# An FFT filter and an ELU block: Z on 128 partitions, its first rows asked for early, weights cast by transfers, late loads in two parts

## The chip, the cores and the metric

The kernel runs on one core of one Trainium2 chip. Its engines are TensorE (PE; PEld in the profile is its weight load), VectorE (DVE), ScalarE (ACT), GpSimd (POOL) and SyncE (SP). Each takes its instructions strictly in its own order. DMAs are issued from SP's queue or from POOL's. The metric is the device time of one execution in microseconds (us); lower is better.

## The reference

```python
X = np.fft.rfft(x, axis=1)                     # x: 8 x 3008 x 256
Yr = Xr @ w_r - Xi @ w_i + b_r                 # 256 x 256 weights
Yi = Xr @ w_i + Xi @ w_r + b_i
Y = shrink(Yr, 0.01) + 1j * shrink(Yi, 0.01)   # sign(v) * max(|v| - 0.01, 0)
y = np.fft.irfft(Y, n=3008, axis=1)            # -> 24064 tokens x 256
h = y @ w_in                                   # 256 x 2048
g = np.where(h > 0, h, np.exp(np.minimum(h, 0)) - 1)
out = g @ w_out                                # 2048 x 256
```

## The kernel before

3008 is 47 times 64, so each transform is done in two matrix stages with constant matrices M1 to M4 that the kernel computes itself at the start (iotas on POOL, range reduction on DVE, Sin on ACT). A batch goes through these units:

- **A**: six units per batch. M1 times x (three tiles `xts[ci]`, two units each); the result `A` is written to a buffer `DA` in DRAM and read back in another layout as `Z`.
- **X**: eight units, eight matmuls each (`M2`, 96 columns) over `Z`. Unit u takes group g = u // 2 of eight slots of Z and half dt = u % 2 of the features. The result is evacuated to `XT` by ACT or DVE. `Z` lies on 96 partitions: (j, h, c), j from 0 to 23; it has one buffer.
- **M**: `XT` times `wcat_r` and `wcat_s` (the complex weights side by side), bias, and the shrinking to `Y`, on DVE with POOL, or in the first batch on ACT with DVE by turns. There, a bias is either added from `bias_bc` by DVE or put into PSUM by a matmul of ones with `bias_p`, which holds the bias as three bf16 parts in rows 0, 32 and 64.
- **B**: M3 times `Y`, written to `DB` in DRAM and read back as `Bs`.
- **Y**: M4 times `Bs`, giving `yT`, the transposed tokens.

Tokens then go through `front` (h = `w_in_s` times `yT`, then Exp on ACT), `elu`/`finish_elu` (POOL and DVE make `gT`), and `back` (`gT` times `w_out_r`, summed over 16 tiles of the hidden size in `ps_o`). One step i of the main loop is one pair of hidden tiles for 512 tokens: 8 pairs per block, 376 steps. The order is written out by hand: `plan(b)` puts the units of batch b+1 (and A of batch b+2) between the steps of batch b, and PE, busy with `front` and `back`, runs them in that order. The first ten steps (`FILL`) use single PSUM banks and carry the units A 1 to 5 of batch 1 and the rest of the first batch's Y.

The opening, before step 0, is the first batch alone, in this order: constants and six A units (with `idle_pe` matmuls, whose results aren't used, between and after them), Z in four slices of eight slots, eight X units, then M by halves (`first_M`, q = 3, 4, 5, 0, 1, 2) with B 3, 4, 5, 0 between them. For B 0 to 2 of the first Bs, a turn inside PE (`turn_B`, `turn_back`) replaces the way through DRAM; rows 48 to 96 of that Bs come by a DMA. `split_B`, `first_Y` and step 0 follow.

The bulk loads: x of batch 1 (three loads of 1 MB) and half of `w_out` (1 MB) go out on POOL's queue behind `gate(Z_of[0][:, 8, 0:1])`, a tiny POOL copy that waits for the second slice of Z; the other half of `w_out` behind a gate on the first `Bs`. `w_in` comes in four quarters as float32 on SP's queue, and DVE scales each to bf16 by 2/S (L727), half a quarter at a time, between the units. `w_r` and `w_i` come as float32 on SP's queue and POOL makes the four parts of `wcat_r` and `wcat_s` of them (L659 to L662).

PSUM in the opening: `pre2` has two double banks (A, X, B), `pre1` four single banks (M and the idle matmuls).

## Time and profile before

| | us |
|---|---|
| median of 3 runs (907.12 to 908.94) | 907.5 |
| the profiled execution, whole | 911.15 |
| the profiled execution, span | 909.3 |
| busy in the span: PE / DVE / ACT / POOL | 887.4 / 719.7 / 696.1 / 325.1 |
| first X matmul | 22.38 |
| first M matmul | 31.71 |
| first B matmul | 39.03 |
| first turn-back matmul | 51.01 |
| first matmul of step 0 | 53.88 |
| first X matmul of batch 1 | 77.11 |

The times of events are from the start of the span. A line such as `PE xps L183 <- DVE XT L126: 1.7, 1, 1.7` reads: PE stood idle before the instruction of line 183 that writes `xps`, until DVE's instruction of line 126 that writes `XT` was done; 1.7 us in all, one time, the longest 1.7. In the chain of waits, each line is a start, a length, and the engine, tile and line that the end of the work can be followed back through. In a table by stretches, the columns are the stretch, its length, an engine's busy time (and its instructions), the granted PE clock as a share of full speed, the share of the DMA engines' time, and GB/s. L126 and L128 are the copies of the helper `evac`, on DVE and ACT.

### The profile page before, as it was taken

What the parts mean: (1) busy time and instruction counts of PE and PEld (TensorE: products, weight loads), DVE (VectorE), ACT (ScalarE), POOL (GpSimd) and SP (SyncE); (2) the same over time, 40 slices, a digit from 0 to 9 for tenths busy, and PEclk for the clock granted to TensorE, in tenths of its full rate; (3) what the DMA queues carried; (4) which work ended last, traced back from release to release, by engine and by line L of the source; (5) the groups of instructions that cost most, each with busy time, mean ns of one, the idle gap of its engine ahead of it and who ended that gap; (6) DMA issues with size and microseconds to landing.
All of it is one profiled execution on the core that took longest, in us unless ns stands there. A gap on an engine that the chain in (4) does not pass through costs nothing.

```text
span 909.3 us, 17311 instructions
## 1 busy us (share of the span) xinstructions
PE 887.4 (98%) x6664; PEld 654.4 (72%) x6767; DVE 719.7 (79%) x908; ACT 696.1 (77%) x869; POOL 325.1 (36%) x457
## 2 busy tenths in 40 slices
PE   8898999999999999999999999999999999999997
PEld 3467667876678766886678766787667867777776
DVE  8687778887788778897788877888778877778776
ACT  6577778778878778787787788878887877767664
POOL 7552441233321341405404154032332134443665
PEclk9799999999999999999999999999999999999999
DMA  8977225721283214732266032752228011231011
GB/s 270 296 216 237 74 71 157 238 70 48 70 243 128 71 47 136 195 112 76 64 194 200 26 93 60 210 172 62 78 65 237 25 43 51 73 91 48 24 47 47
DMA packets 90655, 106.06 MB, mean 117 GB/s; under 512 B 5302, under 2 KB 81340, under 8 KB 87212
## 3 DMA queue, kind: packets, MB, share of 16 engines
q1 hardware_dynamic: 84316, 77.42, 30.5%
q0 software_dynamic: 5968, 27.26, 9.0%
q8 instruction: 53, 0.87, 0.4%
q10 hardware_dynamic: 288, 0.26, 0.1%
q14 instruction: 30, 0.25, 0.1%
HBM read 55.12 MB, written 49.81 MB: 115 GB/s over the span
## 4 chain that ended last, share of the span: by engine, by line
PE 85%; DVE 4%; ACT 3%; DMA 3%; issue 2%; POOL 1%; SPq 0%; DVEq 0%; ACTq 0%; POOLq 0%
PE ps_o L945 34%; PE hps L871 33%; PE mps L200 9%; PE bps L252 2%; PE yps L420 2%; PE xps L183 2%; PE aps L150 2%; DMA Z<-DA 1%; DVE gT L915 1%; DVE Et L926 1%; ACT Et L889 1%; ACT Et L892 1%; DMA xt<-in_x_dram 1%; ACT Bz L265 1%; DMA Bs<-DB 0%
## 5 line engine op out<-in xcount | busy, mean ns | idle before, releaser
L945 PE MATMUL ps_o<-w_out_r,gT 128*128 128x256 f32 x3008 | 475.3, 301 | 0.7 <-DVE gT L913 0.7
L945 PEld LDWEIGHTS ps_o<-w_out_r,gT 128*128 128x128 f32 x3008 | 402.9, 189 | 49.8 <-DVE osb L957 1.4
L871 PE MATMUL hps<-yT,w_in_s 128*128 128x512 bf16 (+7 forms) x1613 | 371.9, 350 | 5.9 <-DVE gT L913 1.0
L913 DVE SCALAR_TENSOR_TENSOR gT<-Et,hps 128x512 fp32r<-128x512 f32 (+1 forms) x268 | 220.2, 851 | 74.4 <-POOL Et L924 38.1
L915 DVE SCALAR_TENSOR_TENSOR gT<-hps,Et 128x1024 fp32r<-128x1024 f32 x190 | 232.4, 1223 | 14.9
L871 PEld LDWEIGHTS <-w_in_s 128*128 128x128 bf16 x1728 | 141.8, 98 | 129.0 <-issue 21.5
L924 POOL TENSOR_SCALAR Et<-Et 128x512 f32<-128x512 f32 x204 | 121.5, 615 | 230.9 <-ACT Et L887 218.6
L892 ACT ACTIVATE Et<-hps 128x1024 f32<-128x1024 f32 x190 | 195.8, 1031 | 9.7 <-PE hps L871 3.5
L926 DVE TENSOR_SCALAR Et<-Et 128x1024 f32<-128x1024 f32 x190 | 131.5, 692 | 47.9 <-ACT Et L892 40.4
L218 POOL TENSOR_SCALAR clip<-yb 128x512 f32<-128x512 f32 x84 | 51.7, 615 | 314.5 <-DVE yb L210 282.3
L887 ACT ACTIVATE Et<-hps 128x512 f32<-128x512 f32 x182 | 98.9, 595 | 62.4 <-PE hps L871 60.9
L889 ACT ACTIVATE Et<-hps 128x1024 f32<-128x1024 f32 x84 | 86.3, 1027 | 71.5 <-PE hps L871 70.0
L219 POOL TENSOR_TENSOR Y<-yb,clip 128x512 bf16<-128x512 f32 x84 | 107.2, 1277 | 7.0
L890 ACT ACTIVATE Et<-Et 128x1024 f32<-128x1024 f32 x84 | 88.8, 1058 | 2.6
L210 DVE TENSOR_TENSOR yb<-mps,bias_bc 128x512 f32<-128x512 f32 x89 | 61.3, 689 | 37.2 <-PE mps L200 24.8
L128 ACT CAST XT<-xps 128x768 bf16<-128x768 f32 x61 | 48.8, 799 | 17.9 <-PE xps L183 17.9
L200 PE MATMUL mps<-wcat_r,XT 128*128 128x512 bf16 x180 | 56.7, 391 | 0.8 <-ACT Bz L265 0.3
L200 PE MATMUL mps<-wcat_s,XT 128*128 128x512 bf16 x182 | 55.9, 385 | 0.7
L200 PEld LDWEIGHTS <-XT 128*128 128x128 bf16 x384 | 31.2, 99 | 30.9 <-issue 2.7
L128 ACT CAST A<-aps 128x1024 bf16<-128x1024 f32 x42 | 42.5, 1014 | 13.1 <-PE aps L150 11.7
L128 ACT CAST yT<-yps 128x752 bf16<-128x752 f32 x56 | 44.2, 789 | 10.4 <-PE yps L420 10.3
L265 ACT CAST Bz<-bps 128x1024 bf16<-128x1024 f32 x45 | 45.1, 1001 | 2.7 <-PE bps L252 2.7
(146 smaller groups left out, 466.7 us busy)
## 6 DMA issues: line engine op xcount, KB each, us to landing
xt<-in_x_dram POOLq DMA_DIRECT2D x21, 1024.0 KB, 7.1
out_dram<-osb SPq DMA_DIRECT2D x158, 128.0 KB
Bs<-DB SPq DMA_DIRECT2D x30, 384.0 KB
DA<-A SPq DMA_DIRECT2D x20, 512.0 KB
DB<-Bz SPq DMA_DIRECT2D x20, 512.0 KB
Z<-DA SPq DMA_DIRECT2D x7, 1152.0 KB
Z<-DA SPq DMA_DIRECT2D x11, 384.0 KB
xt<-in_x_dram POOLq DMA_DIRECT2D x6, 512.0 KB, 5.9
```

The lines of the kernel that those rows point to most:

```text
L128: nc.scalar.copy(dst, src)
L200: nc.tensor.matmul(ps, lhsT=XT[:, dt, c, o : o + P], rhs=wm[:, dt, :], start=(not biased and m == 0 and dt == 0), stop=(m == 1 and dt == 1),)
L219: nc.gpsimd.tensor_tensor(Y_of[b, q][:, i, :], yb, clip[:], ALU.subtract)
L871: nc.tensor.matmul(hps[s][:, c0:c1] if early else hps[:, s, c0:c1], lhsT=w_in_s[:, dt, ft * P : ft * P + P], rhs=yT_of[b][:, dt, t0 : t0 + ...
L887: nc.scalar.activation(E_[:, s], hps[:, s], AF.Exp)
L889: nc.scalar.activation(E_, hps[:], AF.Relu, scale=-1.0)
L892: nc.scalar.activation(E_, hps[:], AF.Exp)
L913: nc.vector.scalar_tensor_tensor(o, e, -1.0, h, ALU.add, ALU.max)
L915: nc.vector.scalar_tensor_tensor(o, h, 0.0, e, ALU.max, ALU.add)
L924: nc.gpsimd.tensor_scalar(E_[s], E_[s], 1.0, 0.0, ALU.min, ALU.max)
L926: nc.vector.tensor_scalar(E_, E_, 1.0, -1.0, ALU.min, ALU.add)
L945: nc.tensor.matmul(po[q][:, i_ % 2, :], lhsT=gT[:, s, i_ * P : i_ * P + P], rhs=w_out_r[:, ft, :], start=(ft == 0 and i_ % 2 == 0), stop=( ...
```

## The change

- `Z0` has 128 partitions and is the one Z of all batches. Of rows 0 to 31 (j from 0 to 7, which the first third of A writes), slot groups 0 and 2 go to partitions 0 to 31, and groups 1 and 3 to partitions 96 to 127, by two DMAs of their own (`load_Z(b, None, None)`); rows 32 to 95 go by the loads as before. Partitions 0 to 31 of groups 1 and 3 are cleared once by ACT. X units of odd groups use all 128 partitions, those of even groups 96; M2 is computed for 128 partitions.
- In the first batch, the two early DMAs are issued right behind the last A write, ahead of its landing; in the others likewise, behind the last A write's issue.
- `w_r` and `w_i` are cast to bf16 by DMAs of POOL's queue behind a gate on the last A tile, and `wcat_s` is made from `wcat_r`. POOL's operations for M4 move behind their issue. `w_in` comes in two halves, cast by DMAs of POOL's queue into `w_in_s`; the factor 2/S goes into M4's weights, and `scale_w_in` is gone.
- The bulk loads: behind the Z gate `w_in`'s first half, x(1,0), x(1,1), `w_out`'s first half; behind the Bs gate `w_in`'s second half, `w_out`'s second half, x(1,2).
- The bias is split on eight partitions by POOL, goes through DRAM (`bpd`) to the rows of `bias_p`, and `bias_bc` is made by a matmul and an ACT copy.
- X of the first batch has three double banks; DVE takes units 2, 4 and 7 instead of 1, 4 and 7; w3's subtraction is behind unit 2, the Abs behind unit 7. 34 idle matmuls instead of 40 ahead of X, three instead of eight within it. In the first batch, M takes the feature half 0 of both weights first.

```diff
@@ -55,7 +55,7 @@
...
     M1 = constp.tile([P, P], F32R, name="M1")
-    M2 = constp.tile([2 * NR, NS, 2, 2 * K1], BF16, name="M2")
+    M2 = constp.tile([P, NS, 2, 2 * K1], BF16, name="M2")
     M3 = constp.tile([P, K1 // 2, 2, P], BF16, name="M3")
...
@@ -84,9 +84,9 @@
     xtp = ctx.enter_context(tc.tile_pool(name="xtp", bufs=1))
...
     ctx.enter_context(tc.manual_schedule())
-    first, second = ExitStack(), ExitStack()
-    pre2 = first.enter_context(tc.tile_pool(name="pre2", bufs=2, space=bass.MemoryType.PSUM))
-    pre1 = first.enter_context(tc.tile_pool(name="pre1", bufs=4, space=bass.MemoryType.PSUM))
+    zeroth, first, second = ExitStack(), ExitStack(), ExitStack()
+    pre2 = zeroth.enter_context(tc.tile_pool(name="pre3", bufs=3, space=bass.MemoryType.PSUM))
+    pre1 = zeroth.enter_context(tc.tile_pool(name="pre0", bufs=2, space=bass.MemoryType.PSUM))
...
@@ -166,10 +166,17 @@
...
-        if b not in Z_of:
-            Z_of[b] = zp.tile([2 * NR, NS, D], BF16, name="Z", tag="Z")
+        Z_of[b] = Z0
         dv = DA_of[b].rearrange("j (h c s) d -> (j h c) s d", h=2, c=2)
-        nc.sync.dma_start(Z_of[b][:, s0:s1, :], dv[:, s0:s1, :])
+        if s0 is None:
+            for t in range(2):
+                dst, src = (
+                    v.rearrange("p (g t s) d -> p g t (s d)", t=2, s=8)[:, :, t]
+                    for v in (Z0[96 * t : 96 * t + 32], dv[0:32])
+                )
+                nc.sync.dma_start(dst, src)
+        else:
+            nc.sync.dma_start(Z0[32:96, s0:s1, :], dv[32:96, s0:s1, :])
...
         g, dt = u // 2, u % 2
@@ -180,9 +187,10 @@
         psv = ps[:].rearrange("p a (k j) -> p (a k) j", j=P)
...
             k = 8 * g + kk
+            r = slice(0, P if g % 2 else 2 * NR)
             nc.tensor.matmul(
-                psv[:, kk, 0 : 4 * K1], lhsT=Z[:, k, dt * P : dt * P + P],
-                rhs=M2[:, k].rearrange("p c m -> p (c m)"), start=True, stop=True,
+                psv[:, kk, 0 : 4 * K1], lhsT=Z[r, k, dt * P : dt * P + P],
+                rhs=M2[r, k].rearrange("p c m -> p (c m)"), start=True, stop=True,
             )
...
@@ -195,12 +203,14 @@
         o = (2 * q + i) * P
...
             nc.tensor.matmul(ps, lhsT=busy[:, 0:P], rhs=bias_p[:], start=True, stop=False)
-        for m, (c, wm) in enumerate(((0, wcat_r), (1, wcat_s))):
-            for dt in range(2):
-                nc.tensor.matmul(
-                    ps, lhsT=XT[:, dt, c, o : o + P], rhs=wm[:, dt, :],
-                    start=(not biased and m == 0 and dt == 0), stop=(m == 1 and dt == 1),
-                )
+        todo = [(c, dt) for c in range(2) for dt in range(2)]
+        if b == 0:
+            todo.sort(key=lambda z: z[1])
+        for c, dt in todo:
+            nc.tensor.matmul(
+                ps, lhsT=XT[:, dt, c, o : o + P], rhs=(wcat_r, wcat_s)[c][:, dt, :],
+                start=(not biased and (c, dt) == (0, 0)), stop=((c, dt) == (1, 1)),
+            )
         if i == 0:
...
@@ -434,15 +444,17 @@
         for _ in range(n):
...
-    brow, rest = (wk3.tile([P, 2 * D], F32, name="yb", tag="yb") for _ in range(2))
-    nc.vector.memset(brow[:], 0.0)
-    for o, bv in ((0, b_r), (D, b_i)):
-        for k in range(3):
-            nc.sync.dma_start(
-                brow[32 * k : 32 * k + 1, o : o + D],
-                bass.AP(tensor=bv.tensor, offset=bv.offset, ap=[[0, 1], [1, D]]),
-            )
+    nc.vector.memset(bias_p[:], 0.0)
+    bpd = dram.tile([3, 2 * D], BF16, name="bpd", tag="bpd")
+    Z0 = zp.tile([P, NS, D], BF16, name="Z")
     idle_pe(9)
+    gatep = ctx.enter_context(tc.tile_pool(name="gatep", bufs=2))
+
+    def gate(src):
+
+        t = gatep.tile([P, 1], F32, name="gate", tag="gate")
+        nc.gpsimd.tensor_copy(t[0 : src.shape[0], :], src)
+
     xts = []
...
         pcol = iota("pcol", [P, 1], [[0, 1]], cm=1)
+        offs = row("offs", [P, 1])
+        nc.gpsimd.memset(offs[:], 0.0)
+        nc.gpsimd.memset(offs[2 * NR : P, :], float(-NR))
+
+        def clear(g):
+            nc.scalar.activation(
+                Z0[0:32, 8 * g : 8 * g + 8, :].rearrange("p s d -> p (s d)"),
+                busy[0:32, 0:1].to_broadcast([32, 8 * D]), AF.Copy, scale=0.0,
+            )
+
         srow = iota("srow", [P, 2 * NS], [[0, 2], [1, NS]])
...
@@ -538,25 +565,28 @@
         dve.tensor_scalar(r1[:], v1[:], 0.25, CMAGIC, ALU.mult, ALU.add)
...
         dve.tensor_tensor(v1[:], r1[:], v1[:], ALU.add)
+        clear(1)
         nc.scalar.activation(r1[:], v1[:], AF.Sin, bias=0.0, scale=TURN / 4.0)
+        clear(3)
...
-        pool.tensor_scalar(idm[:], prow, pcol[:], None, ALU.is_equal)
-
+        for k in range(3):
+            pool.tensor_copy(bps[:, k], bsm[:])
+            if k < 2:
+                pool.tensor_tensor(bsm[:], bsm[:], bps[:, k], ALU.subtract)
         def fA(u):
...
             if u < 5:
@@ -646,6 +669,7 @@
         wraps(0)
...
             fA(u)
+        nc.sync.dma_start(bpd[:].rearrange("k (q e) -> q k e", q=8), bps[:])
         points(1)
...
         points(2)
@@ -654,19 +678,28 @@
         wraps(1)
...
         fA(5)
-        nc.sync.dma_start(w_r_f[:], w_r.rearrange("(c p) e -> p c e", p=P))
-        nc.sync.dma_start(w_i_f[:], w_i.rearrange("(c p) e -> p c e", p=P))
-        pool.tensor_copy(wcat_r[:, :, 0:D], w_r_f[:])
-        pool.tensor_copy(wcat_r[:, :, D : 2 * D], w_i_f[:])
-        pool.tensor_scalar(wcat_s[:, :, 0:D], w_i_f[:], -1.0, None, ALU.mult)
-        pool.tensor_copy(wcat_s[:, :, D : 2 * D], w_r_f[:])
+        gate(A_of[0, 2][:, 7, 0:1])
+        for o, wv in ((0, w_r), (D, w_i)):
+            nc.gpsimd.dma_start(
+                wcat_r[:, :, o : o + D], wv.rearrange("(c p) e -> p c e", p=P)
+            )
+        ph4 = col(pool, c4, 0.25, ALU.mult, 0.25, ALU.add)
+        k4s = col(pool, k4, 1.0 / N1, ALU.mult)
+        wn = col(pool, qcol, 0.0, ALU.is_equal, -0.5, ALU.mult)
+        wc = col(pool, wn, 1.0, ALU.add, 2.0 / S, ALU.mult)
+        pool.tensor_tensor(w41[:], wc[:], c1[:], ALU.mult)
+        pool.tensor_tensor(w40[:], wc[:], c0[:], ALU.mult)
+        pool.tensor_scalar(v4[:], arow, k4s[:], ph4[:], ALU.mult, ALU.add)
+        pool.tensor_scalar(r4[:], v4[:], CMAGIC, -CMAGIC, ALU.add, ALU.add)
+        pool.tensor_tensor(v4[:], v4[:], r4[:], ALU.subtract)
+        pool.tensor_scalar(idm[:], prow, pcol[:], None, ALU.is_equal)
+        pool.tensor_copy(wcat_s[:, :, D : 2 * D], wcat_r[:, :, 0:D])
+        pool.tensor_scalar(wcat_s[:, :, 0:D], wcat_r[:, :, D : 2 * D], -1.0, None, ALU.mult)
+        load_Z(0, None, None)
+        for k in range(3):
+            nc.sync.dma_start(bias_p[32 * k : 32 * k + 1, :], bpd[k : k + 1, :])
         for g in range(4):
             load_Z(0, 8 * g, 8 * g + 8)
-        for o, bv in ((0, b_r), (D, b_i)):
-            nc.sync.dma_start(
-                bias_bc[:, o : o + D],
-                bass.AP(tensor=bv.tensor, offset=bv.offset, ap=[[0, P], [1, D]]),
-            )
         sines(0, 0)
...
@@ -698,63 +731,54 @@
         dve.scalar_tensor_tensor(
...
         )
-        idle_pe(40)
-
-    gatep = ctx.enter_context(tc.tile_pool(name="gatep", bufs=2))
+        idle_pe(34)
+
     late2 = ctx.enter_context(tc.tile_pool(name="late2", bufs=2))
...
     w_out_v = moe_w_out.rearrange("(t p) e -> p t e", p=P).bitcast(F32R)
-    FQ = DFF // 4
-    w_in_f = []
-
-    def load_w_in(q):
-        if q < 3:
-            wf = late3.tile([P, 2, FQ], F32, name="w_in_f", tag="Et")
-        else:
-            wf = late2.tile([P, 2, FQ], F32, name="w_in_f", tag="osb")
-        nc.sync.dma_start(wf[:], w_in_v[:, :, q * FQ : q * FQ + FQ])
-        w_in_f.append(wf)
+    def load_w_in(hh):
+        hf = slice(hh * DFF // 2, (hh + 1) * DFF // 2)
+        nc.gpsimd.dma_start(w_in_s[:, :, hf], w_in_v[:, :, hf])
...
-    def scale_w_in(q, on_dve, c=slice(0, 2)):
-        dst = w_in_s[:, c, q * FQ : q * FQ + FQ]
-        if on_dve:
-            nc.vector.tensor_scalar_mul(dst, w_in_f[q][:, c], 2.0 / S)
-        else:
-            nc.scalar.activation(dst, w_in_f[q][:, c], AF.Copy, scale=2.0 / S)
-
-    def gate(src):
-
-        t = gatep.tile([P, 1], F32, name="gate", tag="gate")
-        nc.gpsimd.tensor_copy(t[0 : src.shape[0], :], src)
-
+    def load_late():
+        load_w_in(1)
+        load_w_out(1)
+        load_x(1, 2)
...
+    gate(Z_of[0][:, 8, 0:1])
     load_w_in(0)
-    gate(Z_of[0][:, 8, 0:1])
-    for ci in range(3):
+    for ci in range(2):
         load_x(1, ci)
...
     nc.vector.tensor_scalar(w3[:], v3[:], CMAGIC, -CMAGIC, ALU.add, ALU.add)
-    nc.vector.tensor_tensor(w3[:], v3[:], w3[:], ALU.subtract)
-    nc.scalar.copy(bias_p[:], brow[:])
-    nc.vector.tensor_tensor(rest[:], brow[:], bias_p[:], ALU.subtract)
+    nb = pre1.tile([P, 512], F32, name="ips", tag="mps1")
     for u in range(8):
-        unit_X(0, u, alone=True, on_dve=u in (1, 4, 7))
+        unit_X(0, u, alone=True, on_dve=u in (2, 4, 7))
+        if u == 0:
+            nc.tensor.matmul(nb[:], lhsT=busy[:, 0:P], rhs=bias_p[:], start=True, stop=True)
         if u == 1:
-            nc.scalar.activation(a3[:], w3[:], AF.Abs)
-            nc.vector.tensor_copy(bias_p[32:64], rest[32:64])
-            nc.vector.tensor_copy(bias_p[64:P], rest[64:P])
-            nc.vector.tensor_tensor(rest[64:P], rest[64:P], bias_p[64:P], ALU.subtract)
-            nc.vector.tensor_copy(bias_p[64:P], rest[64:P])
-        idle_pe(1)
+            nc.scalar.copy(bias_bc[:], nb[:])
+        if u == 2:
+            nc.vector.tensor_tensor(w3[:], v3[:], w3[:], ALU.subtract)
+        if u in (1, 3, 5):
+            idle_pe(1)
+    nc.scalar.activation(a3[:], w3[:], AF.Abs)
+    zeroth.close()
+    pre2, pre1 = (
+        first.enter_context(
+            tc.tile_pool(name=n_, bufs=k_, space=bass.MemoryType.PSUM, reuse_waits="tile")
+        )
+        for n_, k_ in (("pre2", 2), ("pre1", 4))
+    )
     for o, src, sc, bi in ((1, w3, TURN, 0.0), (0, a3, -TURN, hpi[:])):
...
@@ -774,36 +798,30 @@
     first_M(4, 1, True)
...
     fB(3)
-    load_w_in(1)
     first_M(5, 1, True)
...
     fB(4)
-    scale_w_in(0, True, 0)
     first_M(0, 1, True)
...
     load_Bs(0, 0, 16 * NT)
-    scale_w_in(0, True, 1)
     first_M(1, 1, True)
...
     turn_B(0)
-    scale_w_in(1, True, 0)
     first_M(2, 1, True)
     fB(0)
-    load_w_in(2)
     turn_B(1)
...
     store_B()
-    load_w_in(3)
     M4v = M4[:].rearrange("p (a h) -> p a h", h=2)
...
     gate(Bs_of[0, 0][64:96, 0, 0:1])
-    load_w_out(1)
+    load_late()
     first.close()
...
@@ -1014,10 +1031,8 @@
                     (load_Bs, (n1, w, 0, 4 * K1 - 16 * (b == w == 0))) for w in range(4)
...
             if u == ("A", 5) and n2 < B:
-                f1[t] += [(load_Z, (n2, s0, s1)) for s0, s1 in ((0, 8), (8, NS))]
+                f1[t] += [(load_Z, (n2, s0, s1)) for s0, s1 in ((None, None), (0, 8), (8, NS))]
         if b == 0:
-            for t in range(4):
-                f1[t + 1].append((scale_w_in, (2 + t // 2, True, t % 2)))
             for t, u in ((1, 1), (3, 2), (4, 3), (5, 4), (6, 5)):
...
             for t, a, u in (
@@ -1026,8 +1041,8 @@
                 a[t].append((split_Y, (0, u)))
...
                 f1[t].append((load_Bs, (0, w)))
-            f1[6] += [(load_Z, (1, s0, s1)) for s0, s1 in ((0, 8), (8, NS))]
-            f1[xs[0]].append((lambda: gate(Z_of[1][:, 16, 0:1]), ()))
+            f1[6] += [(load_Z, (1, s0, s1)) for s0, s1 in ((None, None), (0, 8), (8, NS))]
+            f1[xs[0]].append((lambda: gate(Z_of[1][:, 28, 0:1]), ()))
         if n2 < B:
```

## The prediction, made before the result was known

> **What bounds the kernel now.** I read the page first, then the chain of waits, the table by stretches, and the waits of TensorE (PE) by stage.
>
> The page (busy time, and the clock by slices of 22.7 us):
> ```profile
> PE 887.4 (98%) x6664; PEld 654.4 (72%) x6767; DVE 719.7 (79%) x908; ACT 696.1 (77%) x869; POOL 325.1 (36%) x457
> PEclk9799999999999999999999999999999999999999
> ```
> PE is busy nearly throughout, and only the second slice (22.7 to 45.5 us) has a lower clock. The waits of PE after 90 us, longest first:
> ```profile
> PE yps L420 <- DMA Bs<-DB: 1.0, 1, 1.0
> PE bps L252 <- ACT Bz L265: 0.2, 1, 0.2
> ```
> So 820 of 909 us can't change: the change takes nothing from PE there. It must win or lose in the first 90 us. The chain there (start, length):
> ```profile
> 23.90 1.10 DVE yb L748
> 25.00 0.88 DVE XT L126
> ...
> 25.92 0.68 PE xps L183 x8
> ...
> 31.53 0.97 DVE XT L126
> ...
> 32.55 1.46 PE mps L200 x3
> ...
> 34.23 2.94 PE mps L200 x8
> ...
> 39.97 1.73 PE mps L200 x8
> ...
> 44.34 0.55 DVE w_in_s L727
> ```
> Z lands and PE starts X at 22.38, but DVE is still at constants and the bias (L748), so PE waits for its evacuation of XT. The same eight matmuls take 2.94 us at 34 us and 1.73 at 40. The waits (20 to 36 us, then 76 to 90 us) and the stretches (length, PE busy, clock, DMA share, GB/s):
> ```profile
> PE xps L183 <- DVE XT L126: 1.7, 1, 1.7
> ```
> ```profile
> PE xps L183 <- DMA Z<-DA: 1.3, 2, 0.9
> ```
> ```profile
> 22.68:26.09 3.41, 1.65 (x28) 1.00 1.02 253
> 26.09:29.50 3.41, 3.08 (x27) 0.50 1.07 344
> 29.50:32.92 3.42, 3.09 (x20) 0.50 1.05 414
> 32.92:36.33 3.41, 3.19 (x8) 0.50 1.09 405
> 77.29:80.70 3.41, 2.40 (x27) 1.00 1.01 257
> ```
> The gap of 1.7 us (24.3 to 25.9) is followed by 10.24 us at half clock, until 36.33. A stretch with 2.40 of 3.41 us busy kept the clock, one with 1.65 lost it.
>
> **The change, part by part.** The sum is made on the profiled execution (span 909.34 us, run 911.15); the median of the other runs is 907.5, which is 3.65 lower, and I subtract the same difference there.
>
> *Start.* Two more memsets on POOL ahead of the first x load (0.09 to 0.10 each): +0.2 us on all that follows. The two clears of Z run on ACT between its first activation (ends 2.22) and the first A copy (6.85). By 0.51 us for 384 elements and 0.85 for 768, 2,048 elements make about 2 us each; 4.1 fit into 4.6 with the 0.26 us sine. Uncovered they would cost 0.5 at most. POOL's bias splits (five tiny operations, about 0.2 each) end before the fourth A copy (12.2), so SP isn't held there. Operations on 128 instead of 96 lanes have the same length per lane: nothing.
>
> *Z.* The last A write is issued at 15.07, and SP waits until 18.41 for its landing. Into that wait of 3.0 us go two early Z loads and three bias rows (about 0.35 each, 1.8 together): hidden. The four later slices carry 256 KB instead of 384. Z's first slice landed 3.87 us after issue; at 1.13 MB in 20 to 24 us (284 GB/s), 128 KB less is 0.46 us. First X: 18.61 + 3.87 - 0.46 = 22.0, against 22.38. The early Z loads and the cast weights (1 MB) may still be moving then: bounds 21.3 to 23.0. Six idle matmuls fewer (0.213 each) end at 21.5 instead of 22.5, a gap of about 0.5 us.
>
> *X stage.* Three double banks instead of two, no L748 (1.10) ahead of DVE's first XT, no L753 to L756 (2.23 together), L746 (0.96) behind it. With 0.80 us per ACT and 0.96 per DVE evacuation, 0.62 for the new bias copy on ACT: ACT does units 0, 1, bias, 3, 5, 6 and ends at 27.55; DVE does 2, w3, 4, 7 and ends at 27.95. Before, unit 7 ended at 32.49: 4.5 us gained. PE's longest gap is then about 0.9 us, and a stretch of 3.41 us has 2.0 us or more busy, between the two rows above but nearer the one that kept the clock: I take full clock.
>
> *M and B.* ACT goes on with Abs 0.84 and two sines 0.85 and 0.93 (to 30.2); DVE with M3's halves 0.95 each, yb 0.69 twice, Y 0.68, to 33.3, where the first B starts at 33.4. Before it was at 39.03: 5.6 us gained. PE then has 2.6 us per pair as before (39.03, 41.62, 44.22). The `w_in` scaling leaves DVE: 0.55 us of it stood on the chain at 44.34; the rest was beside other work. Turn-back starts at 44.9 instead of 51.0: **-6.1 us**. The `wcat_s` casts on POOL (0.6 to 3.1 us each before) end by about 24 and are needed at 27.6.
>
> *FILL blocks.* Four scalings fewer on DVE in the first five blocks (0.41 to 0.79 each, mostly hidden): **-0.3**. Against it: `x(1,2)` is now the last of three 1 MB loads behind the Bs gate on POOL's queue. The gate opens at about 45.2 and the first is issued at 45.6. A lone 1 MB x load took 5.3 to 5.5 us, two together landed 2.5 apart. In the trace's packets 1 MB of w_out cost the engines 4.0 us, x 2.7, w_in about 3.3, and SP's traffic beside them (DB and DA) 3.7: 13.7, in 52 to 62 us done 1.13 to the microsecond (11.25 in 10), so 12.1. With the 2.6 us of a lone load that aren't movement (5.3, the shortest, less 2.7) it lands at 60.3. Unit A(1,4) needs it 13.9 us after turn-back (64.87 against 51.0), at 58.5. Bounds: 56.5 (no sharing, no stall) to 63 (the casts at half speed). **+1.7**. `w_in`'s second half, first in line, lands at 52 and is needed at 55.0: covered by 3 us; the first half has 20.
>
> One rule speaks against this part: the Trainium skill (SBUF — State Buffer, "A bandwidth-pool intuition that's wrong", its warning on DMAs from GpSimd) says that such a DMA's descriptors can't be written while DVE runs a two-port operation. Here four such issues at 25.05 to 27.96, with DVE busy 1.9 of 2 us, took 0.62 to 1.01 us each and show nothing of it. By that rule, with a DVE operation of 0.7 us ahead of each of three issues, the time would be up to 2.1 us more.
>
> *Z of batch 1.* A third of its load goes with the last A write, and the remaining 1 MB is less than 1.57. The waits of 0.4 and 0.95 us (and a weight load held 0.2 longer) at 77.1 and 83.6 go: **-1.4**. What is late next there is DVE's gT (1.0 us at 78.6), which stays. Two more issues per batch on SP later stand ahead of output writes (0.3 to 0.4 each), which nobody waits for.
>
> Sum: -6.1 - 0.3 + 1.7 - 1.4 = -6.1; span 903.2, run 905.0, median **901.4**.
>
> **Rivals.**
> *The clock still drops in X* (thin matmuls, five idle or bias ones instead of eight): for, the X stage has 62% busy and where a stretch of 3.41 us begins isn't known. X is bound by evacuation, so the loss is in M: three groups at 1.8 instead of 0.9, less 1.0 us that PE would have waited there: about +2. 903.4. A page differs here: the Trainium skill (TensorE: Matmul & The Clock Gate, Part 1) has the clock fall after an idle window of about 3.4 us. The row has it fall with half that idle, so the measurement decides; by the page this rival would have no chance.
>
> *The late loads cost nothing:* SP's traffic barely shares, x lands by 58.5. -7.8, 899.7.
>
> *Little is gained:* Z's first slice waits behind the early 512 KB and the casts (23 us), the clock drops too, and x stalls: 905.5 to 907.5.
>
> *Slower:* the casting loads move far below the x loads. At a quarter of the speed `w_in`'s half takes 12 us instead of 3: it lands at 60.6 (5.6 late), x at 68 (4.1 more), and such a stall costs the clock (one or two stretches of 3.41 at half: 1.7 to 3.4): +12.3 - 6.1 - 0.3 - 1.4 = +4.5, 912. It decides from where x lands more than 18 us after the gate. For: no load of before changes its type, so the trace shows no such speed. Against: w_out, with eight times shorter rows than x, cost only half more.
>
> **How the numbers follow.** Forecast 0.58, clock drop 0.15, no late cost 0.10, little gained 0.08, slower 0.09. The 80% range takes in Z's bounds, the late loads and the clock drop: 897.5 to 907.0. About 0.2% (1.8 us) is what a measurement of this kernel tells from no change; with half of "little gained" within it: faster 0.85, same 0.05, slower 0.10.
>
> **What would show it.** Right: the first XT of DVE at about 23, the granted clock 1.00 in 24 to 37 us, M from 27.6, the first B at 33 to 34, turn-back at 45, a PE wait at the fifth A unit of batch 1 for an x landing near 60, no wait for Z at 70 to 78 us. Wrong: a clock of 0.5 after 22 us, a first X after 23, PE waiting on `w_in_s`, or any new wait after 90 us.

## The result

The changed kernel took 910.13 us against 907.63 before (medians): a ratio of 1.0029, interval 1.002 to 1.0038. It is slower by 0.29%, where 901.4 us and a gain were forecast.

The profiled execution of that comparison had a granted clock of 0.75 from end to end and can't be laid beside the profile of before, so the profile after is one of the same kernel run again (`e1_changed`: span 908.1, run 909.91, median 909.15).

The page of the profile after, its busy line and its clock line:
```profile
PE 888.2 (98%) x6757; PEld 652.6 (72%) x6757; DVE 710.6 (78%) x896; ACT 699.8 (77%) x871; POOL 327.9 (36%) x467
PEclk9999999999999999999999999999999999999999
```
PE is as busy as before (888.2 against 887.4), and no slice stands out in its clock. The waits of PE in 20 to 36 us and in 50 to 70 us, the longest of each, and the longest after 90 us:
```profile
PE xps L191 <- issue: 2.6, 1, 2.6
```
```profile
PE gps L150 <- DMA xt<-in_x_dram: 2.2, 1, 2.2
```
```profile
PE yps L430 <- DMA Bs<-DB: 1.2, 1, 1.2
```
The first is PE idle between the last idle matmul (ends 22.07) and the first X (24.64); this profile names no releaser for it ("issue"), and in e4 and e7 below the same wait is put down to `Z<-DA`. The second is new: the fifth A unit of batch 1 waits for x(1,2). The third was there before. The chain of waits (start, length):
```profile
16.27 5.84 DMA Z<-DA
22.11 2.53 issue
24.64 0.51 PE xps L191 x8
25.18 1.50 ACT XT L128 x2
...
36.09 1.73 PE mps L210 x8
...
50.68 12.25 DMA xt<-in_x_dram
63.07 0.71 PE gps L150 x2
63.78 1.39 PE ps_o L962 x8
65.17 1.73 PE sps L888 x4
...
68.95 0.86 PE sps L888 x4
```
DVE's constants and bias have left the chain at X; Z's transfer stands there instead, with the 2.53 us behind it. M runs at 1.73 us per eight matmuls from its start. Then comes the late x load, 12.25 us from issue to landing, and behind it four matmuls of `front` take 1.73 us instead of 0.86. The table by stretches (length, PE busy, then the other engines, the clock, DMA share, GB/s) tells why:
```profile
26.09:29.50 3.41, 2.85 (x47) 2.12 (x45) 2.96 (x4) 3.41 (x6) 2.94 (x5) 1.00 0.56 62
32.92:36.33 3.41, 2.99 (x20) 1.35 (x19) 2.85 (x5) 2.57 (x4) 3.15 (x4) 1.00 1.06 425
64.06:67.47 3.41, 3.41 (x12) 2.30 (x11) 1.64 (x3) 1.24 (x4) 0.61 (x1) 0.50 1.04 326
```
In this execution the X and M stages keep the full clock, as forecast. The half clock is now behind the wait for x.

### The profile page after: what moved, and what is told of

It is laid out like the page before. It is cut to its first block, busy times and chain, and to the rows that moved or that the text cites. A ratio compares the mean times of both kernels' runs of the same rounds, so it can differ in the third digit from the quotient of the medians.

```text
span 1111.7 us, 17305 instructions
## 1 busy us (share of the span) xinstructions
PE 1092.2 (98%) x6654; PEld 764.6 (69%) x6757; DVE 719.2 (65%) x896; ACT 712.7 (64%) x871; POOL 327.8 (29%) x467
## 4 chain that ended last, share of the span: by engine, by line
PE 97%; issue 1%; DMA 1%; DVE 1%; POOL 0%; ACT 0%; DVEq 0%; POOLq 0%
PE ps_o L962 39%; PE hps L888 37%; PE mps L210 9%; PE bps L262 3%; PE xps L191 2%; PE yps L430 2%; PE aps L150 2%; PE ips L445 1%; PE sps L888 1%; DMA xt<-in_x_dram 1%; PE gps L150 0%; DVE gT L930 0%; PE mps L205 0%; PE gps L416 0%; POOL xt L117 0%
## 5 line engine op out<-in xcount | busy, mean ns | idle before, releaser
L962 PE MATMUL ps_o<-w_out_r,gT 128*128 128x256 f32 x3008 | 576.6, 344 | 0.0
L962 PEld LDWEIGHTS ps_o<-w_out_r,gT 128*128 128x128 f32 x3008 | 482.0, 210 | 83.5 <-issue 51.2
L888 PE MATMUL hps<-yT,w_in_s 128*128 128x512 bf16 (+7 forms) x1613 | 468.0, 422 | 8.7 <-DVE gT L930 1.0
L888 PEld LDWEIGHTS <-w_in_s 128*128 128x128 bf16 x1728 | 160.3, 110 | 177.2 <-issue 144.3
L932 DVE SCALAR_TENSOR_TENSOR gT<-hps,Et 128x1024 fp32r<-128x1024 f32 x190 | 232.4, 1223 | 15.2 <-DVE Et L943 0.5
L210 PE MATMUL mps<-wcat_s,XT 128*128 128x512 bf16 x182 | 70.8, 457 | 1.3
L210 PE MATMUL mps<-wcat_r,XT 128*128 128x512 bf16 x179 | 68.7, 459 | 0.5 <-DVE XT L126 0.3
L210 PEld LDWEIGHTS <-XT 128*128 128x128 bf16 x384 | 35.2, 110 | 39.8 <-issue 20.9
L128 ACT CAST A<-aps 128x1024 bf16<-128x1024 f32 x42 | 42.4, 1012 | 23.4 <-PE aps L150 23.3
```

The lines of the kernel that those rows point to most:

```text
L128: nc.scalar.copy(dst, src)
L210: nc.tensor.matmul(ps, lhsT=XT[:, dt, c, o : o + P], rhs=(wcat_r, wcat_s)[c][:, dt, :], start=(not biased and (c, dt) == (0, 0)), stop=((c ...
L888: nc.tensor.matmul(hps[s][:, c0:c1] if early else hps[:, s, c0:c1], lhsT=w_in_s[:, dt, ft * P : ft * P + P], rhs=yT_of[b][:, dt, t0 : t0 + ...
L932: nc.vector.scalar_tensor_tensor(o, h, 0.0, e, ALU.max, ALU.add)
L962: nc.tensor.matmul(po[q][:, i_ % 2, :], lhsT=gT[:, s, i_ * P : i_ * P + P], rhs=w_out_r[:, ft, :], start=(ft == 0 and i_ % 2 == 0), stop=( ...
```

## The experiments

Sixteen kernels were run. Those of one set shared a chip and the runs of before; the sets lay on different chips (but for the first and the last), so ratios to before are compared across sets. One profile is one execution: the issue of the last A write alone varied from 15.07 to 17.26 us between them.

### First set: the suspects one at a time

`e1_changed` is the changed kernel itself.

> The changed kernel itself, for a profile at full clock. The one at hand had a granted clock of 0.75 over its whole span, but its transfers tell something: first X at 24.9 (forecast 22.0), x(1,2) landed at 66.3 (forecast 60.3). Theory L (late loads): at full clock PE reaches the fifth A unit of batch 1 at about 61 and waits there 4 to 6 us for x(1,2), and a wait of that length brings the granted clock to 0.5 for at least one stretch of 3.4 us; without the two the kernel would be 3 to 5 us faster than before. Theory Z (late first slice): there is no such wait; turn-back starts at 49 to 51 and the whole gain was lost ahead of it. Rival C (clock): the granted clock is 0.5 for 7 to 14 us around X, as before. Time by all of them as measured, 908 to 913, ratio about 1.003.

It took 909.15 (before 907.5), ratio 1.0019 (1.001 to 1.0027). Its profile has the wait of theory L and one stretch at half clock behind it, but 2.2 us of waiting instead of 4 to 6. Turn-back was at 47.28, ahead of theory Z's 49 to 51, and the clock was full around X, against rival C.

`e2_x_early` puts the third x load back behind the Z gate:
```diff
-        load_x(1, 2)                  # load_late
-    for ci in range(2):
+    for ci in range(3):
         load_x(1, ci)
```


> One part undone: all three x loads of batch 1 go out behind the Z gate as before the change, so that only the second halves of w_in and w_out are behind the Bs gate. Theory L: the wait of PE at the fifth A unit goes, and the time falls 3 to 6 us below the changed kernel (904 to 907, ratio 0.996 to 0.999). Theory Z: no wait to lose, within 1 us of the changed kernel. Rival C: the same within 1 us, with the clock of the X stage unchanged.

It took 906.83, ratio 0.9995 (0.9986 to 1.0004). In its profile the fifth A unit doesn't wait, and the clock is full throughout. The late x load cost 2.3 us of the median, less than the 3 to 6 of theory L.

`e3_w_ungated` issues the casting loads of `w_r` and `w_i` right behind the last x load of batch 0:
```diff
-        gate(A_of[0, 2][:, 7, 0:1])
-        for o, wv in ((0, w_r), (D, w_i)):   # behind fA(5)
-            nc.gpsimd.dma_start(...)
+        for o, wv in ((0, w_r), (D, w_i)):   # behind batch 0's x loads
+            nc.gpsimd.dma_start(...)
```


> The casting loads of w_r and w_i are issued on POOL's queue right behind the last x load of batch 0 (about 7 us) instead of behind the gate on the last A tile, so that they are done before the early Z loads move. Theory Z: half of the 2.9 us by which the first X is late is theirs, first X at 23 to 23.5 instead of 24.9, time 1 to 1.5 us below the changed kernel; the price may be a last A write that lands up to 1 us later. Theory L: first X moves but PE loses the gain at the fifth A unit, whose x lands at a time that hangs on the gate: less than 1 us of change.

It took 907.51, ratio 1.0003 (0.9994 to 1.0012). The first X came 6.94 us after the issue of the last A write, instead of 8.84. But that issue was itself at 17.25 instead of 15.80, behind a stretch at half clock among the A units (11.7 to 15.2 us), so X was only 0.45 us earlier. The wait for x was 1.7 us, without a half clock behind it. The time is 1.6 us below the changed kernel, about what theory Z had, but only a part of that is seen at the first X.

`e4_Z_on_96` undoes the Z part: 96 partitions, four slices of 384 KB, nothing early, no clears.
```diff
-        if s0 is None: ...            # two early DMAs
-        else:
-            nc.sync.dma_start(Z0[32:96, s0:s1, :], dv[32:96, s0:s1, :])
+        if s0 is not None:
+            nc.sync.dma_start(Z0[0:96, s0:s1, :], dv[:, s0:s1, :])
-            r = slice(0, P if g % 2 else 2 * NR)
+            r = slice(0, 2 * NR)
```


> The Z part undone: Z on partitions 0 to 95, four slices of 384 KB behind the last A write's landing and none early; everything else as changed. Theory Z (the early 512 KB stand in the first slice's way): first X comes at 22.5 to 24 and the time is 0 to 2 us below the changed kernel. By the forecast's own step (the first slice is 128 KB smaller, so 0.46 us sooner, and the waits of 1.4 us at batch 1's X go): 2 us slower than the changed kernel. Theory L: within 1 us, but for the 1.4 us at batch 1's X.

It took 910.69, ratio 1.0038 (1.0025 to 1.005). The first X came as late as in the changed kernel (8.88 us behind the last A write's issue against 8.84), so the early DMAs are not what holds the first slice. From first X to first M it took 6.08 us instead of 4.76, but with a stretch at half clock in it:
```profile
24.73:28.14 3.41, 3.41 (x35) 2.78 (x34) 0.62 (x1) 2.09 (x3) 2.32 (x5) 0.50 0.64 140
```
The changed kernel, with Z on 128 partitions, took 6.06 us there when it had such a stretch (e14, below), so these 1.3 us are the clock's. By the medians of this set Z on 128 partitions is a gain of 1.5 us, not a loss, though the two intervals overlap a little and the changed kernel's first measurement (1.0029) lies within that of e4. All five runs had a granted clock of 0.997 or less, and four of the eleven of e1. Why Z on 96 should lose the clock more often isn't shown: PE waits for no later slice in this profile.

### Second set: the base, the weights, and the two repairs together

`e5_before_again` is the kernel before, unchanged, for a profile at full clock.

> The kernel before, unchanged, for a profile in which the granted clock stays up. Theory (the base of the forecast was not the usual execution: its 10.24 us at half clock, 26.09 to 36.33, are missing in ordinary runs): the clock is 0.99 to 1.00 in 22 to 45 us, the first X again near 22.4, the first M near 30.5 to 31.7, the first B near 36.5 instead of 39.03, the turn-back near 48 instead of 51.0, and the span is 905 to 907 instead of 909.3. Rival (the half clock is there in every run and the shortfall lies all in the changed kernel): the clock is 0.5 from about 26 to 36 us again, first B near 39, turn-back near 51, span about 909.

The first theory held (span 906.0, run 907.77):
```profile
core 0: 906.0 us, clock 1.000
```
Its chain and its stretches show M at the speed that the forecast thought only the change would give:
```profile
32.63 1.73 PE mps L200 x8
34.57 1.73 PE mps L200 x8
```
```profile
26.09:29.50 3.41, 2.02 (x28) 1.33 (x28) 3.27 (x6) 1.84 (x3) 2.65 (x4) 1.00 1.02 250
29.50:32.92 3.42, 2.98 (x26) 1.53 (x26) 2.77 (x4) 2.36 (x3) 0.00 (x0) 1.00 1.07 420
```
First B at 36.23 instead of 39.03, turn-back at 48.26 instead of 51.01. Of 112 runs of before with a recorded clock, 110 had 0.998 or more; the profile that the forecast was made on had 0.993.

`e6_x_early_w_f32` is x early and, besides, `w_r` and `w_i` as float32 on SP with POOL's four casts:
```diff
-        gate(A_of[0, 2][:, 7, 0:1])
-        for o, wv in ((0, w_r), (D, w_i)): ...
+        nc.sync.dma_start(w_r_f[:], ...)
+        nc.sync.dma_start(w_i_f[:], ...)
+        pool.tensor_copy(...)         # and the three others
```


> The changed kernel with two parts undone: all three x(1,.) loads behind the Z gate, and w_r and w_i loaded as float32 on SP's queue behind the last A write, with POOL's four casts, as before. Theory (the casting loads of w_r and w_i, 2.0 to 2.3 us of engine time each beside Z's first slice, hold that slice up by 1 to 1.8 us): the first X comes at 22.4 to 23.2 instead of 24.14, all that follows to the turn-back 1 us earlier, and the time is 0.5 to 1.3 us below the kernel with x early alone (906.83), 905.5 to 906.3; ratio to before 0.998 to 0.9995. Rival (the early Z loads and the bias rows hold the slice): first X still at 24.0 or later and about the same 906.8. Second rival: POOL's casts, now after the float32 weights land, come late for M (they end after 28 us), and M starts later than 28.9 though X is earlier.

It took 911.03, ratio 1.0048 (1.0035 to 1.006): the theory and both rivals missed. The first X was at 23.41 (7.91 us behind the last A write), somewhat earlier, and M at 28.19. But POOL ran its casts and then, as this edit left them, the operations for M4, so the Z gate opened at 28.93 instead of 25.02 (x early alone), and all bulk loads were that much later. They met the writes of `DB`: SP waited 7.3 us for one to land, `Bs` was issued at 49.69 instead of 45.62 (in e7 below), and PE stood still:
```profile
PE one L403 <- issue: 3.9, 1, 3.9
```
Two stretches at half clock followed (52.05 to 58.87). So this run doesn't price the cast by itself; with the Z gate 4 us later, the kernel lost more than an earlier X could bring.

`e7_x_early_w_ungated` has the edits of e2 and e3 together.

> The changed kernel with all three x(1,.) loads behind the Z gate and the casting loads of w_r and w_i right behind the last x load of batch 0, without a gate. Alone, the first took 2.3 us from the changed kernel's time and the second 1.6. Theory (they act at different places: the second at the first Z slice, the first at the fifth A unit of batch 1): first X at about 24.2 as with the second alone, A units of batch 1 without a wait, clock 1.00; but the second's gain lay in the late loads, which started 0.4 us earlier, so hardly more than x early alone: 906.5 to 906.9. Rival (they add): 905.2 to 905.6.

It took 905.09 (before 906.79), ratio 0.9984 (0.9975 to 0.9993): the first version to beat before. In ratios it lies between the theory (0.9995, x early alone) and the rival (both effects taken off 1.0019 give 0.9979). The first X was 7.24 us behind the last A write, no A unit waited, and the 81st `back` matmul was at 78.88 (before at full clock 81.44, changed 83.25).

### Third set: where each part counts

`e8_e7_Z_on_96` is e7 with the Z part undone as in e4.

> The kernel with x early and w_r, w_i ungated, and in it the Z part undone: 96 partitions, four slices of 384 KB, nothing early, no clears. Theory (Z on 128 partitions is a gain by itself, in the later slices of batch 0: the changed kernel took 1.32 us less from its first X to its first M than the kernel with Z on 96): from first X to first M 6.0 to 6.6 us instead of 5.22, and 0.8 to 1.6 us more in all, 906.0 to 906.7. Rival (without the casting loads beside Z the four slices come in time either way): the same 5.2 us, and the time within 0.4 us of 905.1. A third: Z on 128 costs (two more DMAs and three rows on SP), and the time falls below 904.6.

It took 906.93, ratio 1.0001 (0.9992 to 1.0009), with 6.48 us from first X to first M: the theory's numbers. Z on 128 partitions is again worth about 0.17%, 1.5 us. But these 6.48 us hold a stretch at half clock as well (25.66 to 29.08), behind one with 1.29 us busy, and waits of 0.4 and 0.2 us for later slices. How much of the 1.5 us is the slices and how much the clock isn't separated.

`e9_before_x_late` is before with the x part alone:
```diff
-    for ci in range(3):
+    for ci in range(2):
         load_x(1, ci)
     load_w_out(1)
+    load_x(1, 2)
```


> The kernel before with one part of the change alone: x(1,2) moved from behind the Z gate to behind the Bs gate, as the last of two loads (w_out's second half, then x). In its profile at full clock the fifth A unit of batch 1 ran at 62.13, and w_out's second half, issued at 49.76, landed at 60.11. Theory (the stall is set by when x lands against when PE comes): x is issued at about 50.7 and lands at 62 to 63, so the wait is 0.3 to 1 us and the clock stays: 907.1 to 908.3, ratio 1.0003 to 1.0013. Rival (what was lost in the changed kernel is a matter of the three casting and other loads together, not of x's place): x lands by 61.5, no wait, ratio 1.000. Second rival: a wait of over 1.5 us with the half clock behind it, and 909 or more.

It took 908.63 (before 907.34), ratio 1.002 (1.001 to 1.003), between the theory and its second rival. x landed at 61.20, and PE waited in this profile for an evacuation (0.8 us, at the same unit), not for x. So the move costs the old kernel 1.3 us as well. Against e5, its profile (run 908.99) loses 0.5 us from the first to the 41st `back` matmul and 0.7 from there to the 81st, where the waits for Z of batch 1 are 2.0 us instead of 1.0. What the slower runs lose isn't shown.

`e10_late_x_first` changes only the order of the three late loads of the changed kernel:
```diff
-        load_w_in(1); load_w_out(1); load_x(1, 2)
+        load_x(1, 2); load_w_in(1); load_w_out(1)
```


> The changed kernel with only the order of the three late loads changed: x(1,2), then w_in's second half, then w_out's second half. Theory (the three cannot all be in time: the first to be issued lands 6.5 us after its issue, each other about 2.5 to 5 later): x lands near 55, seven microseconds before its use, and w_in's half lands at 58 to 60 where step 4 needs it at 57.5, so the wait is there, at hps or sps for w_in_s, 0.5 to 2.5 us long, and the time is 907 to 908.6, between the changed kernel (909.15) and the one with x early (906.83). Rival (it is only x's place at the end): no wait for w_in_s, and the time of x early, 906.4 to 906.9.

It took 908.37, ratio 1.0012 (1.0003 to 1.002). The profile (run 906.32) shows x at 52.80, `w_in`'s half at 56.66, and no wait of PE for either (one weight load was held 0.3 us for `w_in`): there the theory was wrong, and the median lies in its range (907 to 908.6) for another reason. For 7 of its 11 runs had a granted clock of 0.997 or 0.998 and took 908.3 to 909.5; the four at 0.999 or 1.000 took 906.2 to 907.5. What the other runs lose goes with the clock.

### Fourth and fifth set: where the clock goes

`e11_x_first_idle44` and `e12_e7_idle44` are e10 and e7 with ten more idle matmuls ahead of X, to close PE's gap there:
```diff
-        idle_pe(34)
+        idle_pe(44)
```


> The kernel with the late x load first of three, with 44 idle matmuls ahead of X instead of 34 (10 more of 0.213 us). Its profile, at a granted clock of 1.000, took 906.3 and showed no wait for w_in_s, but 7 of its 11 runs had a clock of 0.997 or 0.998 (one or two stretches of 3.41 us at half) and took 908.3 to 909.5. Theory (what costs those runs the clock is PE's gap ahead of the first X, 1.7 us in the profile between the last idle matmul's end at 21.86 and X at 23.54): the gap falls to under 0.5 us, nearly all runs have 0.999 or 1.000, and the median is 906.2 to 907.2. Rival (the clock goes at another place, at w_in_s or at the fifth A unit in runs where a load lands later): as many runs at 0.997 and 0.998 as before, median 908 to 908.6.

> The kernel with x early and w_r, w_i ungated, with 44 idle matmuls ahead of X instead of 34. Two of its 11 runs had a clock of 0.997 (905.85 and 907.23), the others 0.999 or more. Theory (the gap of 1.1 us ahead of X costs the clock in few runs): those runs are gone, the median moves by 0 to -0.4, 904.7 to 905.1, and no run is above 906.2. Rival (where Z's first slice lands early, the idle matmuls, now ending near 24.2, hold X up): +0.3 to +0.9, 905.4 to 906.

They took 909.82, ratio 1.0024 (1.0014 to 1.0034), and 908.24, ratio 1.0002 (0.9991 to 1.0013): worse, against the theory. Yet in the profile of e12 the opening was no slower (the 81st `back` matmul at 78.95, in e7 at 78.88), and in that of e11 it was slower by only 0.6 us (79.82, in e10 79.25). Most of the loss came 700 us later, in 770 to 800 us (e12's lines; e11 waits 2.3 us there and has the same half clock):
```profile
PE yps L430 <- DMA Bs<-DB: 2.9, 1, 2.9
```
```profile
791.19:794.60 3.41, 0.54 (x7) 0.35 (x6) 1.67 (x3) 0.69 (x2) 1.19 (x2) 1.00 0.98 270
794.60:798.01 3.41, 3.19 (x17) 2.48 (x19) 0.00 (x0) 1.71 (x2) 0.00 (x0) 0.50 0.67 166
```
The last batch's first `Bs` is short of time in every kernel (0.6 to 2.9 us of waiting in the profiles), and behind the two longest, 2.3 and 2.9 us, a stretch at half clock follows.

The last set takes that wait away in four kernels alike, by two empty slots ahead of the last batch's first two Y units:
```diff
-                seq += [("A", 5), ("n", 0), ("n", 1)]
+                seq += [("A", 5)] * (1 if n2 < B else 3) + [("n", 0), ("n", 1)]
```


> The kernel before, with the first two Y units of the last batch two steps later (two empty slots), 4.3 us behind where they stood. Theory (PE's wait for the last batch's first Bs, 1.0 us in both profiles of before, goes, and nothing takes its place): no wait at yps in 770 to 800 us, ratio 0.9985 to 0.9995, 906.3 to 907.1 where before has 907.6. Rival (the wait only moves, to another unit of the last batch): ratio 1.000.

> The changed kernel with the first two Y units of the last batch two steps later. Theory A (the changed kernel's loss lies in the opening: 1.4 us at the first X, 3.4 at x(1,2) with the half clock behind it, less 2.8 in X and 0.6 at the second Z): it stays 1.5 to 2.5 us above before with the same slack, 908 to 909.5. Theory B (a part of it is the tail: in some runs the wait of the last batch runs over 2 us there and the clock halves): the difference to before with the same slack shrinks to under 1 us, and no run is above 910.

> The kernel with x early and w_r, w_i ungated, with the first two Y units of the last batch two steps later. Alone it was 0.9984 of before. Theory: 0.6 us of wait less in the profile, more in runs with a long wait; 0.9965 to 0.998 of before, about 904.5 to 905.8 where before has 907.6, all runs at 0.998 to 1.000. Rival: no gain over 0.9984.

> The kernel with x early, w_r and w_i ungated and 44 idle matmuls, with the first two Y units of the last batch two steps later. In its profile without that it stood level with the one of 34 idle matmuls up to 79 us (78.95 against 78.88) and lost 4.2 us behind it, 2.3 more of waiting at the last batch's first Bs and a stretch at half clock. Theory (the idle matmuls cost nothing themselves, the tail was chance): within 0.4 us of the kernel with 34 idle matmuls and the same slack. Rival (they delay X in most runs and cost the opening 0.5 to 1 us): 0.6 to 1.2 us above it, also with the slack.

| with the slack | median (before 907.04) | ratio | interval |
|---|---|---|---|
| e13, before | 906.15 | 0.9989 | 0.998 to 0.9997 |
| e14, changed | 907.58 | 1.0008 | 0.9997 to 1.002 |
| e15, e7 | 904.21 | 0.9967 | 0.9955 to 0.998 |
| e16, e7 with 44 idle matmuls | 904.02 | 0.9966 | 0.9954 to 0.9977 |

No profile of the four has a wait at that place. Before gains 0.9 us, and the changed kernel stays 1.4 above it (just under theory A's 1.5 to 2.5); its highest runs are still at 910.0 to 911.0, against theory B. So most of the change's loss is not in the tail but in the opening, though the intervals of e13 and e14 touch. The idle matmuls cost that kernel nothing: e16 and e15 are level, and e12's loss was the tail. e15 and e16 are 0.33% faster than before, 0.21% faster than before with the same slack (e13). The stretches of e14, the changed kernel, show both of its weak places in one execution (run 911.04):
```profile
21.09:24.50 3.41, 0.91 (x6) 0.30 (x5) 1.58 (x3) 0.52 (x1) 3.00 (x5) 1.00 1.04 318
24.50:27.91 3.41, 3.41 (x35) 2.85 (x35) 0.55 (x1) 2.09 (x3) 3.41 (x6) 0.50 0.33 47
62.05:65.46 3.41, 0.66 (x3) 0.60 (x4) 0.32 (x1) 0.71 (x3) 1.19 (x2) 1.00 0.98 275
65.46:68.88 3.42, 3.42 (x14) 2.41 (x13) 1.88 (x3) 1.03 (x2) 0.14 (x1) 0.50 1.08 351
```
Here each stretch in which PE waits (for Z's first slice, for x) is followed by one at half clock.

## Why the prediction was wrong

The ledger by stages, both profiles at full clock but for the changed kernel's one stretch after x:

| from | to | before (e5) | changed (e1) | difference |
|---|---|---|---|---|
| start | last A write's issue | 15.86 | 15.80 | -0.06 |
| | first X | 7.41 | 8.84 | +1.43 |
| | first M | 7.60 | 4.76 | -2.84 |
| | first B | 5.36 | 5.75 | +0.39 |
| | turn-back | 12.03 | 12.13 | +0.10 |
| | first `back` matmul | 5.98 | 5.98 | 0 |
| | 41st `back` matmul | 13.31 | 16.72 | +3.41 |
| | 81st `back` matmul | 13.89 | 13.27 | -0.62 |
| | end | 824.55 | 824.88 | +0.33 |

The sum is +2.14 us, 908.13 less 905.99.

**The base (the step that failed most).** The sum was made on an execution with 10.24 us at half clock, and the page showed this. Ordinary runs don't have it. The forecast's 6.1 us up to turn-back (51.01 to 44.9) fall into three parts: 2.75 were never there to be won (51.01 against 48.26 at full clock), 0.98 were won (48.26 to 47.28), and 2.38 were not reached (47.28 against 44.9).

**"I subtract the same difference there."** The 3.65 us between the profiled run and the median were for the most part that same half clock, so it was counted twice: as a gain of the change and again in the subtraction. For the changed kernel the difference is 909.91 less 909.15, 0.76. That is 2.9 of the 7.75 us between 901.4 and 909.15; the other 4.9 are the 2.4 above, 2.0 at the late loads, and 0.5 in the rest.

*Start* (+0.2) can't be told apart in a last A write that varied by 2 us between executions.

***Z* (first X at 22.0, bounds 21.3 to 23.0).** It was 24.64. The sum gave the first slice 3.41 us from its issue (3.87 less 0.46); in e1 it was 5.74 from that issue to the first X. "128 KB less is 0.46 us" priced the slice and not what moves beside it. Counted from the first slice's issue, the first X came after 4.72 to 5.74 us in the six profiles with `w_r` and `w_i` cast behind the A gate (e1, e2, e4, e10, e11, e14), and after 3.11 to 4.47 us in all others (the one at 0.75 aside), with these weights ungated or as float32. In the traces the first packets of the gated casting loads start at 17.7 to 18.0 us and the last at 21.0 to 23.3, beside the slice. The last of the ungated ones start by 16.3, those of before's float32 loads by 20.0. The engines' time for them differs little: 1.9 to 2.2 us for 512 casting packets (59 to 70 ns each, 512 bytes written), 1.6 for the same weights in float32 (49 to 51 ns for 1 KB). So it is more the place that cost than the cast. The early Z DMAs were hidden, as forecast. Ungated, the last A write was issued at 15.7 to 16.1 us, hardly later than gated (15.5 to 15.8), but at 17.3 in e3 and e15, which had a stretch at half clock among the A units.

***X stage* (right in e1, by a weak argument).** In e1 the clock was full, and the first M came 4.76 us after the first X, where 5.6 was forecast (27.6 less 22.0). But a stretch with 2.0 us busy is nearer to the one with 1.65 that lost the clock than to the one with 2.40 that kept it, not farther, as the forecast had it. The rival of a clock drop in X isn't dead: e4, e8 and e14 had it, behind a late first slice, and e14 took 6.06 us then. How the gain against before is shared among the parts of the change isn't shown; e4's 1.3 us are that drop.

***M and B*.** 5.8 was forecast from the first M to the first B (27.6 to 33.4), 5.75 measured. The 0.55 us of `w_in` scaling "on the chain" at 44.34 brought nothing (first B to turn-back 12.13 against 12.03): behind it, the second halves' clip and Y on ACT and DVE were as late.

***FILL* (+1.7 for the late x, +3.41 in the ledger).** The landing was right, in part by luck: 15.4 us after turn-back forecast, 15.65 measured (47.28 to 62.93), but the gate opened 1.3 us after turn-back instead of 0.3, and from there x took 14.4 us instead of 15.1. `w_in`'s half, forecast to be covered by 3 us, had 2.0. PE's wait was 2.2 us for 1.8. What was missing is the rest, 1.2 us: a stretch at half clock behind the wait. The forecast named that consequence and priced it only in its slower rival. By e2 the whole part is worth 2.3 us of the median. The half clock is not all of that: e1's median run, 909.15, had a granted clock of 1.000. The rival's condition (x more than 18 us after the gate) was not met, with these 14.4 us from the gate (48.54) to the landing, and the kernel was slower without it.

The rule weighed there, that of the Trainium skill (SBUF — State Buffer, "A bandwidth-pool intuition that's wrong") on GpSimd's DMA descriptors and DVE's two-port operations, shows nothing here either: the three late issues took 0.80, 0.90 and 0.60 us, back to back. But DVE ran copies out of PSUM meanwhile, and no run shows whether any of them is a two-port operation, so the rule isn't tested.

***Z of batch 1* (-1.4).** The waits for Z at 74 to 82 us went, 1.0 us in two pieces at full clock, and the stage gained 0.6. The same 0.6 came in e4 without the Z part, whose A units were late; so it isn't shown that the early rows bring it.

**"820 of 909 us can't change."** By the changed work, no: 0.33 us. But the wait that was read there, 1.0 us at `yps`, is a draw between 0.6 and 2.9 us, and taking it away from both kernels was worth 0.9 us in before.

Still open: what the runs of e1 with a granted clock of 1.000 lose, what costs the slower runs of e9 their time, by what Z on 128 partitions gains its 1.5 us, and how much of the wider spread of the changed kernel's runs belongs to each of its two weak places.

## What to carry to other kernels

Look at the clock of the profiled execution before a sum is made on it: if it is lower than in the ordinary runs, a gain that only undoes the low clock isn't there, and the distance to the median can't be subtracted again. Price a wait of PE of about two microseconds or more with the half-clock stretch that may follow (in the profile of before a gap of 1.7 us was enough). A load that is moved must be held against what moves at its new place: gated behind the last A, small casting loads delayed the one slice that the path waited for, and a 1 MB load put last in a queue of three landed 2 us too late, while the third of Z that was moved ahead of the wait held nothing up. Before two profiles are subtracted stage by stage, look whether a stretch at half clock lies in one of them: the 1.3 us that seemed to be the price of Z on 96 partitions were one.

## What the runs showed of the hardware

The half clock comes in stretches of 3.41 us. Against the kernel's own events their starts differ from one execution to the next (26.09, 64.06, 24.73, 24.50, 794.60 us), and each of these stands behind a stretch in which PE was idle for more than half of the time. Laid on its own grid, e1's profile shows one gap split and one whole:
```profile
19.69:23.10 3.41, 2.38 (x12) 0.88 (x9) 2.96 (x8) 1.90 (x4) 3.09 (x6) 1.00 1.14 254
23.10:26.51 3.41, 1.87 (x35) 1.66 (x36) 0.21 (x1) 1.33 (x2) 3.41 (x6) 1.00 0.53 201
60.65:64.06 3.41, 1.17 (x7) 0.93 (x7) 0.87 (x3) 1.34 (x3) 1.19 (x2) 1.00 0.82 236
```
The gap of 2.57 us ahead of X fell into two stretches, 2.38 and 1.87 us busy, and cost no clock; the 2.2 us for x fell into one, 1.17 busy, and did. In e14 the gap ahead of X fell into one (0.91 busy) and did as well. Behind 20 us, stretches followed by a half clock had 0 (e6) to 1.65 us (before) busy of 3.41. The busy time alone draws no sharp line: a stretch with 1.68 (e3, 59.53 to 62.95) kept the clock, and ahead of 20 us one with 1.80 (e3, 8.33 to 11.74) lost it. Such stretches go with a part of the 1 to 3 us by which runs of one kernel differ at a granted clock of 0.995 to 1.000, but not with all of it: two runs of e1 with 1.000 took 909.0 and 909.15. The Trainium skill (TensorE: Matmul & The Clock Gate, Part 1) has the window of 3413 ns run freely, whatever the kernel does, and the runs agree; that it takes an idle window to lose the clock, they don't: one with 1.65 of 3.41 us busy was enough.
